# Attention kernel on one core: the queues of four engines in another planned order

## Chip, core and metric

The kernel runs on one core of a Trainium2 chip. The metric is the device time of one execution in microseconds (us), lower is better. A core has five engines with an instruction queue each, served in order: TensorE (PE, matmuls; PEld is its weight load), VectorE (DVE), ScalarE (ACT), GpSimd (POOL) and SyncE (SP, which here only issues transfers). They wait for each other through semaphores. On-chip data lie in SBUF; matmuls write to PSUM, which has eight banks.

## What is computed

Two attention blocks over S = 2048 positions, D = 1024, H = 32 heads of 32, whose outputs are concatenated:

```python
def _A_ref(x, wqkv, wo):
    qkv = ...                                   # x @ wqkv, split into heads
    scores = jnp.einsum('bhqd,bhkd->bhqk', q, k) * Dh ** (-0.5)
    p = _softmax(scores, axis=-1)
    o = jnp.einsum('bhqk,bhkd->bhqd', p, v)
    return o... @ wo

def _B_ref(x, wq, wk, wv, wo, beta):            # four segments of 512
    for s in range(N):
        logits = jnp.einsum('bhqd,bhkd->bhqk', qs, ks) * scale + mask
        a_dot = jnp.einsum('bhqk,bhkd->bhqd', _softmax(logits), vs)
        pq = phi(qs)
        a_mem = (pq @ M) / (pq @ z + 1e-06)
        o = g * a_mem + (1.0 - g) * a_dot
        M = M + jnp.einsum('bhld,bhle->bhde', phi(ks), vs)
        z = z + sum(phi(ks))
    return o @ wo
```

Block A is full attention; block B is causal attention within a segment plus a linear memory of the segments before.

## The kernel before

**The stream of scores.** Heads are worked on in groups of four (g = 0 to 7 in A). One score row (L1190) is a set of eight or more matmuls, four heads at once in four row tiles of TensorE, that fill four PSUM banks of 512 columns. Banks 0 to 5 form three slots of two; a row takes two slots and ScalarE empties each by one exp (`ACTIVATE P`, L1288). There are 593 pieces of rows and 1184 exps. For about a tenth of the tiles the exp is replaced by a square polynomial: VectorE reads the bank and scales it into Y (L1236, the cube read), GpSimd squares it (Z, L1245) and scales it into Pc (L1246). A row can start when the exps and cube reads of its banks' last contents are done.

**Work with the probabilities.** For each set TensorE multiplies P with V (L1401) and with ones for the row sums (L1408), in column tiles, into one bank of banks 6 and 7. VectorE then transposes the sums (L1515 or L1426), takes reciprocals (L1518), and GpSimd and VectorE scale and transpose the result back (L1533, L1535).

**Jobs.** Between rows TensorE does projections (L829 through `mm4`; L1866 for the first V), the memory of block B and the output products. A projection of a 512-column tile is eight steps over the contraction; each step is two operations of 256 columns (`halves`, L1593), which are emitted as one instruction of 512 columns if they stand next to each other in the queue. A job takes a bank of the pair 6 and 7 (`tenant`, L1576; the choice stands in the string `BANKS`, L26), VectorE evicts it (L1608) and squares it (L1621) for the bound that guards the exps. Changing between row tiles and column tiles is a change of `mode` in the program.

**Transfers.** All loads and stores but four go through SyncE's queue in program order; weights of block A's next pair of projections are loaded by L1544, x is loaded transposed by L1572.

**How the order is made.** `schedule` (L434) lists all operations with planned durations and puts them on five queues by keys, due times and readiness; its result is the starting order. `rearrange` (L606) then applies the table `MOVES` (L201), one string for TensorE, ScalarE, VectorE and GpSimd each. A pair `gap+shift` steps `gap` places on and takes the operation `shift` places behind to the place reached:

```python
for e, text in MOVES.items():
    q, i = queue[e], 0
    for gap, shift in (x.split("+") for x in text.split()):
        i += int(gap)
        q.insert(i, q.pop(i + int(shift)))
```

After it, the waits between tenants of one bank are derived from TensorE's order, and `programs` (L712) writes each queue with its semaphore waits. SyncE has no string, so its order stays that of `schedule`. Semaphore waits follow from the data dependencies, whatever the order.

Of the kernel before, what the change touches and what calls it, by code (L numbers as in the profile page):

```python
# [145 lines left out]
class Op:  # L146
# [17 lines left out]
    def __hash__(self):  # L164
# [50 lines left out]
        "9+1 12+1 1+1 1+1 1+1 1+1 2+8 2+7 5+1 1+1 9+1 4+5 1+5 1+5 1+5 1+6 1+6 1+6 1+6 1+6 1+6 1+5 19+1 1+1 1+1 1+1 2+2 2+1 1+1 "
        "1+1 1+1 1+1 1+1 1+1 1+1 1+1 1+1 1+4 1+1 1+1 1+1 1+1 1+1 1+1 13+11 3+9 1+9 1+2 9+1 6+1 1+1 1+1 1+1 5+1 8+3 1+3 9+18 1+18 "
        "1+18 5+2 12+1 7+2 1+2 1+2 1+3 1+3 1+3 1+2 1+2 1+2 1+2 1+2 1+2 1+2 1+3 1+3 1+3 1+3 1+2 9+1 1+1 1+1 1+1 1+1 4+10 1+10 1+10 "
        "1+10 1+10 1+10 1+5 2+8 3+6 5+3 10+1 1+1 1+1 1+1 1+3 12+5 9+1 1+1 2+5 1+4 1+4 1+4 1+4 1+4 1+4 1+4 1+4 1+4 1+4 1+4 1+4 1+6 "
        "1+4 1+4 1+4 1+4 11+1 1+1 1+1 1+1 1+1 1+1 1+1 1+1 1+1 1+2 1+2 1+5 1+1 1+4 1+4 1+4 1+4 16+1 1+2 1+2 1+2 1+2 3+2 1+2 1+2 "
        "1+2 1+2 1+2 1+2 1+2 2+3 10+1 1+1 1+1 1+1 5+5 1+5 1+5 9+1 1+1 12+1 1+1 1+2 2+1 1+1 1+1 1+1 1+1 1+1 2+2 1+17 12+4 3+3 7+3 "  # L220
        "3+3 7+1 12+7 1+7 1+7 1+5 12+3 11+2 5+2 8+2 1+2 1+2 1+2 1+2 1+2 1+2 1+2 1+2 1+5 1+2 1+2 1+2 1+2 1+2 1+2 1+2 1+2 6+5 1+5 "
        "6+4 1+4 1+4 1+4 1+4 1+5 1+4 1+4 1+4 1+4 1+4 1+4 1+4 1+4 1+4 1+4 1+4 3+4 3+4 5+2 1+2 1+2 1+2 1+2 1+2 1+1 1+1 1+1 1+1 1+1 "
        "1+1 1+1 1+1 1+2 1+2 1+5 2+1 1+1 1+1 4+3 1+3 1+3 1+3 1+3 1+3 3+1 1+1 3+1 1+1 1+1 1+1 1+1 1+1 1+1 1+1 1+1 1+1 1+1 1+1 4+1 "
        "1+1 7+3 2+2 1+2 1+2 1+2 3+5 1+5 3+1 1+1 2+3 1+3 1+3 1+3 2+1 2+1 1+1 1+1 1+18 1+1 1+1 1+1 1+1 1+1 1+1 1+2 1+2 2+1 1+1 1+1 "
        "1+1 1+1 1+1 1+1 1+1 1+1 1+1 1+1 1+1 1+1 2+7 1+7 1+7 1+7 4+4 1+4 1+4 1+4 2+5 1+3 1+3 1+3 1+3 1+3 1+3 2+2 1+2 6+4 2+4 1+4 "
        "1+4 1+4 1+4 1+4 5+3 14+3 5+1 1+1 1+1 1+1 1+1 1+1 2+3 8+3 6+3 5+1 1+1 2+3 3+1 1+1 1+1 1+1 1+1 1+1 1+1 1+1 1+1 1+1 1+4 1+1 "
        "1+1 1+1 1+1 1+1 1+5 7+1 5+4 1+4 1+4 1+4 1+5 1+5 1+5 1+4 1+4 1+4 2+3 1+3 1+3 1+3 2+2 1+2 1+5 6+5 1+5 1+5 1+5 6+4 13+4 6+3 "
        "1+3 1+3 1+3 1+3 1+3 1+5 1+3 1+3 1+3 1+3 1+3 1+3 1+3 1+3 1+3 1+3 1+6 9+1 2+5 7+13 1+13 3+7 7+4 5+5 5+1 4+17 1+17 4+4 14+2 "
        "13+3 3+4 3+2 1+2 1+2 1+2 1+2 2+5 5+1 1+1 1+1 5+7 1+5 5+2 1+2 1+2 1+2 1+2 1+2 1+2 1+2 1+2 1+2 5+1 1+2 1+2 1+2 1+2 11+1 "
        "1+1 1+1 1+1 1+1 1+1 1+1 1+1 4+1 1+1 1+1 1+1 1+1 1+1 1+1 4+4 1+4 1+4 1+4 1+4 1+4 1+4 1+4 1+4 1+4 3+1 2+7 1+7 1+7 4+1 1+1 "  # L230
        "1+1 1+1 1+1 1+1 1+1 3+2 1+2 1+3 3+1 1+1 1+1 1+1 1+1 1+1 4+1 1+1 1+1 1+1 1+1 1+1 10+5 1+5 1+5 1+5 1+1 1+4 1+4 1+5 1+5 3+3 "
        "1+3 13+1 1+1 1+1 1+1 1+1 6+13 1+1 1+1 1+12 1+12 12+1 1+1 9+1 1+1 13+1 1+1 5+2 1+2 1+2 1+2 1+3 1+3 1+2 1+2 1+2 11+1 6+3 "
        "4+3 12+5 11+5 1+10 7+5 1+5 1+5 1+4 1+4 1+4 1+4 1+4 1+4 1+4 1+4 1+4 1+4 1+4 1+4 1+4 1+4 1+4 10+4 1+3 2+3 1+3 1+3 1+3 1+3 "
        "4+12 2+11 2+1 12+1 14+1 6+1 1+1 7+1 1+1 13+1 2+3 1+3 1+3 1+3 1+3 1+3 4+1 7+3 1+3 1+3 1+3 1+3 8+4 1+4 8+14 1+18 1+18 13+7 "
        "1+7 1+7 1+7 1+7 1+7 5+4 1+4 1+2 1+3 1+3 1+3 1+3 1+3 1+3 1+3 1+3 1+2 6+4 1+4 1+4 1+4 1+4 1+4 1+5 1+5 2+6 1+6 1+6 1+6 4+1 "
        "1+2 1+2 2+1 1+1 3+1 1+1 1+1 1+1 1+1 1+10 1+10 8+1 1+1 1+1 1+1 8+1 1+1 1+1 1+1 1+1 1+1 1+1 2+5 1+5 1+5 1+5 1+5 1+5 2+4 "
        "1+4 1+1 1+3 1+3 1+3 1+4 1+4 1+4 1+4 1+4 7+5 1+5 1+5 1+5 2+4 1+4 1+1 3+1 1+1 1+1 1+1 1+1 1+2 1+2 1+2 1+2 1+2 7+1 1+1 1+1 "
        "1+1 1+1 2+15 1+15 1+15 9+1 7+1 1+1 1+1 1+1 1+1 10+9 1+10 1+10 1+10 15+1 1+1 1+1 1+19 1+19 2+18 1+18 11+1 9+1 1+18 1+18 "
# [2046 lines left out]
```

## Time and profile before

| | |
|---|---|
| median of 3 runs | 1057.38 us (1057.37 to 1058.42) |
| span of the profiled execution | 1056.3 us |
| mean granted TensorE clock | 1.000 |
| VectorE busy, idle in front of cube reads | 703.4 us, 110.1 us |
| GpSimd busy | 724.7 us |
| ScalarE: first and last exp | 11.9 us, 1043.6 us (end) |

In the profile's groups a row names the line, the engine, the operation and the tiles (output<-inputs), then busy time, mean duration in ns, and the idle time of the engine directly in front with what ended it. Rows of waits read "who <- for whom: us in total, times, longest"; they list the longer waits alone. Rows of the timeline give start, duration, engine, line, operation, and in brackets the idle time before. Matmuls overlap in the pipeline, so a duration there is longer than the distance to the next start.

### The profile page before, as it was taken

How to read it: one execution, taken by the hardware profiler on the slowest of the kernel's cores; microseconds unless marked ns; L12 is line 12 of the kernel's file. 1: busy time of each engine (PE TensorE's matmuls, PEld its weight loads, DVE VectorE, ACT ScalarE, POOL GpSimd, SP SyncE). 2: the span in 40 equal slices, each digit the busy share in tenths (PEclk: the TensorE clock that was granted, in tenths of full speed). 3: DMA queues.
4: the chain of work that ended last, by engine and by line, in shares of the span. 5: the costliest groups of instructions: out<-in, count | busy, mean ns of one | idle time of the engine just before them, and what ended most of it. 6: DMA issues, size and time to landing. Idle time of an engine off the chain costs nothing.

```text
span 1056.3 us, 54941 instructions
## 1 busy us (share of the span) xinstructions
PE 1023.3 (97%) x25091; PEld 551.2 (52%) x25092; DVE 703.4 (67%) x1451; ACT 1001.5 (95%) x1193; POOL 724.7 (69%) x999
## 2 busy tenths in 40 slices
PE   9999999999999999999999999999999999999998
PEld 4456455566555454556555445556555445445544
DVE  3457577666656878696755879777646887674444
ACT  5999999999999999898999999999999999999995
POOL 1005567666766888888956899888755878985551
PEclk9999999999999999999999999999999999999999
DMA  9213351007112530033241221133041433122002
GB/s 175 47 43 93 68 138 28 16 13 160 49 41 70 123 85 17 3 62 92 67 113 44 78 65 38 27 75 91 27 113 35 125 102 113 33 68 73 28 29 66
DMA packets 172377, 72.24 MB, mean 68 GB/s; under 512 B 135536, under 2 KB 170352, under 8 KB 172144
## 3 DMA queue, kind: packets, MB, share of 16 engines
q1 hardware_dynamic: 169776, 67.93, 26.3%
q8 instruction: 197, 3.23, 1.3%
q10 hardware_dynamic: 2368, 0.79, 0.3%
q14 instruction: 36, 0.29, 0.1%
HBM read 45.36 MB, written 11.80 MB: 54 GB/s over the span
## 4 chain that ended last, share of the span: by engine, by line
PE 56%; ACT 32%; DVE 4%; POOL 3%; SPq 3%; issue 1%; DMA 0%; ACTq 0%; POOLq 0%; DVEq 0%
ACT P L1288 32%; PE ps L829 27%; PE ps L1190 11%; PE ps L1401 8%; PE ps L1408 8%; SPq L1572 2%; POOL Z L1245 2%; DVE Y L1236 1%; PE ps L1866 1%; PE ps L1638 1%; POOL Pc L1246 1%; DVE T L1515 1%; DMA W_A<-in_A_wqkv_dram 0%; DVE PKQ_B L1925 0%; POOL P L1317 0%
## 5 line engine op out<-in xcount | busy, mean ns | idle before, releaser
L1288 ACT ACTIVATE P<-ps 128x1024 bf16<-128x1024 f32 (+1 forms) x1178 | 991.5, 999 | 33.6 <-PE ps L1190 18.7
L1245 POOL TENSOR_TENSOR Z<-Y 128x512 f32<-128x512 f32 x287 | 304.2, 1062 | 202.2 <-DVE Y L1236 177.7
L1408 PE MATMUL ps<-P,onesb 128*32 128x256 bf16 (+1 forms) x4386 | 300.8, 270 | 0.7 <-issue 0.6
L1401 PE MATMUL ps<-P,V_A 128*32 128x256 bf16 x3618 | 257.7, 274 | 0.7 <-issue 0.3
L1236 DVE TENSOR_SCALAR Y<-ps 128x512 f32<-128x512 f32 x239 | 163.7, 685 | 110.1 <-PE ps L1190 90.5
L1190 PE MATMUL ps<-KQ_A 32*128 32x256 bf16 x4096 | 204.1, 272 | 12.4 <-ACT P L1288 5.5
L1246 POOL TENSOR_SCALAR Pc<-Z 128x512 bf16<-128x512 f32 x239 | 155.6, 654 | 11.0 <-PE ps L1190 0.2
L1190 PEld LDWEIGHTS ps<-KQ_A 32*128 32x128 bf16 x4096 | 62.8, 92 | 163.9 <-ACT P L1288 108.7
L1408 PEld LDWEIGHTS ps<-P,onesb 128*32 128x32 bf16 x4386 | 128.8, 96 | 30.1 <-issue 14.8
L829 PE MATMUL ps<-xT_B,W_B 128*32 128x512 bf16 (+1 forms) x2132 | 138.7, 372 | 0.8 <-DVE OT_B L1948 0.2
L829 PE MATMUL ps<-xT_A,W_A 128*32 128x512 bf16 (+1 forms) x2020 | 131.4, 370 | 2.2 <-DMA W_A<-in_A_wqkv_dram 1.1
L1401 PEld LDWEIGHTS ps<-P,V_A 128*32 128x32 bf16 x3618 | 108.1, 96 | 34.3 <-issue 14.3
L1401 PE MATMUL ps<-Pc,V_A 128*32 128x256 bf16 x478 | 123.1, 273 | 0.4 <-ACT P L1288 0.2
L1408 PE MATMUL ps<-Pc,onesb 128*32 128x256 bf16 x478 | 122.8, 273 | 0.0
L1317 POOL TENSOR_SCALAR_AFFINE_SELECT P<-P 128x768 bf16<-128x768 bf16 (+1 forms) x96 | 76.3, 803 | 34.7 <-ACT P L1288 33.1
L1515 DVE STREAM_TRANSPOSE T<-ps 128x512 f32<-128x512 f32 x122 | 86.3, 708 | 14.0 <-PE ps L1408 11.9
L829 PEld LDWEIGHTS ps<-xT_B,W_B 128*32 128x32 bf16 x2132 | 50.3, 96 | 45.5 <-issue 19.6
L829 PE MATMUL ps<-Wo_B,OT_B 128*32 128x512 bf16 (+1 forms) x1080 | 71.6, 370 | 0.2 <-DVE rc L1518 0.2
L829 PE MATMUL ps<-Wv_B,xT_B 128*32 128x512 bf16 (+1 forms) x1096 | 70.3, 367 | 0.2
L829 PEld LDWEIGHTS ps<-xT_A,W_A 128*32 128x32 bf16 x2020 | 47.4, 96 | 42.1 <-issue 12.5
L1533 POOL TENSOR_TENSOR T<-T,rc 128x256 bf16<-128x256 f32 x74 | 48.9, 663 | 29.6 <-DVE rc L1518 25.8
L1608 DVE CAST KQ_A<-ps 128x512 bf16<-128x512 f32 x60 | 41.3, 689 | 40.5 <-PE ps L829 40.1
(109 smaller groups left out, 1201.0 us busy)
## 6 DMA issues: line engine op xcount, KB each, us to landing
Wv_B<-in_B_wv_dram SPq DMA_DIRECT2D x32, 256.0 KB, 3.5
W_B<-in_B_wk_dram SPq DMA_DIRECT2D x32, 256.0 KB, 3.3
W_B<-in_B_wq_dram SPq DMA_DIRECT2D x32, 256.0 KB, 4.1
Wo_B<-in_B_wo_dram SPq DMA_DIRECT2D x32, 256.0 KB, 3.5
out_dram<-outsb SPq DMA_DIRECT2D x56, 128.0 KB, 1.9
W_A<-in_A_wqkv_dram SPq DMA_DIRECT2D x14, 256.0 KB, 3.6
ot_a_scratch<-OTst SPq DMA_DIRECT2D x52, 64.0 KB, 2.3
xT_A<-ot_a_scratch SPq DMA_DIRECT2D x6, 512.0 KB, 4.8
```

The source lines that it names most:

```text
L829: ins = e.matmul(out[r], w[:, r], x, start=start, stop=stop, tile_position=(0, 32 * t), skip_group_check=True)
L1190: ins = e.matmul(out, kap, qap, start=st, stop=True, tile_position=(32 * h, 0), skip_group_check=True)
L1236: o = self.dve(lambda e: e.tensor_scalar(Y[:, :], src, SCALE, MID, ALU.mult, ALU.add), 512, key - 9.0, [self.bank[bank]], [rY], fixed=0.15)
L1245: self.pool(lambda e: e.tensor_tensor(Z[:, :], Y[:, :], Y[:, :], ALU.mult), 512, key, [rY], [rZ], rate=0.58)
L1246: return self.pool(lambda e: e.tensor_scalar(dst, Z[:, :], C2, REST, ALU.mult, ALU.add), 512, key, [rZ], [rP], rate=TS_RATE)
L1288: a = self.act(guarded if early and not free else lambda e: e.activation(dst, src, ACT.Exp, scale=SCALE), cols, key, rd, wr, fixed=EXP_FIXED)
L1317: self.pool(lambda e: e.affine_select(v, v, pattern=pat, compare_op=ALU.is_ge, fill=0.0, base=0, channel_multiplier=-1), 2 * nd * P, key + ...
L1401: ins = e.matmul(self.ps[32 * h:32 * h + 32, 512 * obk + q0:512 * obk + q0 + nq], v, p, start=first, stop=last, tile_position=(0, 32 * h), ...
L1408: ins = e.matmul(self.ps[32 * h:32 * h + 32, lcol + q0:lcol + q0 + nq], self.onesb[:, 0:32], p, start=False, stop=last, tile_position=(0, ...
L1515: self.dve(lambda e: e.transpose(T2[:, :], src), 512, k - NORM_K, [obk.res], [ro, rl], fixed=0.17)
L1533: self.pool(lambda e: e.tensor_tensor(half.rearrange("p (b r) -> p b r", r=32), ov, bc, ALU.mult), QC, k, [ro, rr], [rl], rate=0.435)
L1608: self.dve(lambda e: e.tensor_copy(dst, src), 512, key, [self.at(b)], rdst, fixed=0.155)
```

## The change

The diff has one hunk, the table `MOVES`. All four strings are replaced; the starting order, `BANKS`, every operation and the queue of transfers stay as they were. TensorE's string has 3135 moves where it had 3159, ScalarE's 16 for 26, VectorE's 1238 for 1195, GpSimd's 800 for 771. The first line of each:

```diff
 MOVES = {
     "PE": (
-        "14+1 1+2 1+3 5+1 5+1 6+1 1+3 1+1 1+2 4+3 2+1 3+1 1+3 2+1 1+3 1+4 5+1 1+1 1+1 1+1 1+1 1+1 1+1 1+1 1+1 1+1 1+1 1+1 1+1 1+1 "
...
+        "13+1 2+1 1+2 1+3 1+4 1+5 2+5 2+5 7+3 2+1 1+2 2+1 4+1 2+1 1+1 4+1 3+2 1+3 1+1 1+1 2+1 1+1 1+1 1+1 1+1 1+1 1+1 1+1 1+1 1+1 1+1 "
...
     "ACT": (
-        "6+1 7+3 24+1 1+1 1+1 1+1 1+1 1+1 1+1 1+1 1+1 1+1 1+1 1+1 1+1 1+1 1+1 52+1 1+1 1+1 1+1 1+1 1+1 1+1 1+1 1083+1 "
+        "6+1 9+1 22+1 1+1 65+1 1+1 1+1 1+1 1+1 1+1 1+1 1+1 1+1 1+1 1080+1 "
     ),
     "DVE": (
-        "1+1 1+1 9+1 1+2 15+2 1+1 2+2 4+1 1+1 1+1 1+4 1+1 1+1 2+1 2+1 1+3 1+1 1+1 3+1 2+1 1+1 1+1 1+1 1+6 1+6 1+2 1+5 1+5 1+5 1+8 "
...
+        "1+1 1+2 1+1 1+1 1+1 1+1 5+1 2+1 13+1 2+1 2+2 4+1 1+1 1+1 1+4 1+4 1+1 1+3 1+1 1+1 1+1 1+1 2+1 3+1 2+1 1+1 1+1 1+1 1+1 1+5 1+1 "
...
     "POOL": (
-        "19+2 1+2 6+1 1+1 2+2 2+1 2+1 4+1 1+1 5+2 3+1 2+1 3+1 1+1 3+1 1+1 1+1 5+1 5+3 1+3 1+5 1+3 1+5 1+3 2+4 1+3 1+2 1+3 1+2 4+6 "
...
+        "20+1 1+1 9+2 2+1 1+1 1+2 1+1 1+1 1+1 2+1 1+2 1+1 4+2 3+2 1+2 2+1 1+1 1+1 2+1 1+1 5+2 3+3 1+4 4+1 1+1 1+2 1+2 1+1 1+1 1+3 1+1 "
...
     ),
 }
```

As an example of what it does, TensorE's queue around the score row that starts at 31.78 us: before, the row is followed by four steps of the projection of K for pair 1 with a row-sum product and the last product with V of one set behind them; after, those products and one step of the projection stand in front of the row.

1 line of the change is left out of this document (added), and 339 rows, old and new, of the table MOVES.

## Prediction

> **What bounds the kernel now.** I read the page's busy shares first, then its chain of work that ended last, then the waits of TensorE and ScalarE, then the timeline at the longest of these waits.
>
> ```profile
> span 1056.3 us, 54941 instructions
> PE 1023.3 (97%) x25091; PEld 551.2 (52%) x25092; DVE 703.4 (67%) x1451; ACT 1001.5 (95%) x1193; POOL 724.7 (69%) x999
> PE 56%; ACT 32%; DVE 4%; POOL 3%; SPq 3%; issue 1%; DMA 0%; ACTq 0%; POOLq 0%; DVEq 0%
> L1288 ACT ACTIVATE P<-ps 128x1024 bf16<-128x1024 f32 (+1 forms) x1178 | 991.5, 999 | 33.6 <-PE ps L1190 18.7
> ...
> PE ps L1190 <- ACT P L1288: 7.7, 21, 0.8
> PE ps L1190 <- DVE Y L1236: 3.7, 9, 0.8
> PE ps L1401 <- DVE T L1515: 2.2, 10, 0.4
> PE ps L829 <- DMA W_A<-in_A_wqkv_dram: 1.1, 1, 1.1
> ...
> ACT P L1288 <- PE ps L1190: 18.7, 37, 1.2
> ACT P L1288 <- PE ps L1408: 11.6, 18, 1.6
> ```
>
> Two engines are nearly full and hand work to each other. TensorE is busy for 1023.3 of 1056.3 us, so all its idle time is 33.0 us, some of it the start and the end. TensorE's work ends only with the kernel's tail, so the span is its work plus its idle time: a new order can save the idle time and nothing else. The waits to look at stand in front of the score rows (L1190): 7.7 us where the exp (L1288) still reads the banks, 3.7 us where VectorE's cube read (L1236) does. The other direction, exps that wait for a row, is larger in sum but costs only what it passes on to TensorE. The execution shown has 1056.3 us from first to last instruction; the median of the runs is 1057.38, 1.1 more. I sum against 1056.3 and add 1.1.
>
> This is how a wait before a row looks (TensorE, then VectorE):
>
> ```profile
> 646.26 0.40 PE L1190 MATMUL ps<-KQ_A 32*128 32x256 bf16 x8
> 646.58 0.40 PE L829 MATMUL ps<-PKQ_B,Mb 128*32 128x512 bf16 x4
> 647.82 0.40 PE L1190 MATMUL ps<-KQ_A 32*128 32x256 bf16 x8 [0.83 <-DVE Y L1236]
> 648.14 0.29 PE L1401 MATMUL ps<-P,V_B 128*32 128x256 bf16 x4
> 648.26 0.28 PE L1408 MATMUL ps<-P,onesb 128*32 128x256 bf16 x4
> ...
> 647.02 0.65 DVE L1236 TENSOR_SCALAR Y<-ps 128x512 f32<-128x512 f32 x1
> ```
>
> The row at 647.82 may not overwrite its bank before the cube read ends at 647.67. One small matmul stood in front of it, and 0.83 us passed with nothing, although the product with V (L1401) and the row sums (L1408) at 648.14 come straight behind it.
>
> **The change part by part.** I played the old and the new table on the same starting queues and compared where each operation stands. No operation is added or removed. TensorE: 3590 of 7344 stand elsewhere; the 593 score rows keep their order. VectorE: 1099 of 1427; GpSimd: 777 of 995; ScalarE: 21 of 1196. The DMA queue on SyncE has no table, so no transfer passes another. BANKS is not in the diff, and each PSUM bank has the same tenants in the same order under both tables: "pool banks planned anew" has no counterpart, and costs and brings nothing.
>
> First term, waits that get work. Between 40 and 1040 us I find 67 score rows with a TensorE gap of over 20 ns in front, 14.6 us together (the 21 and 9 waits above are the longer ones). In the new order 31 of them have more work ahead, 9 less, 27 the same; over all 577 rows of that stretch it is 226, 160 and 191. So the work went where the trace idles, by 3.4 to 1 against 1.4 to 1. At 647.82, the product and row sums at 648.14 and 648.26 move in front: 0.22 us of the 0.83. Adding the smaller of gap and added work, row by row, gives 4.1 us. The other 70 gaps of TensorE (9.1 us, such as L1401 waiting for the transpose L1515) give 2.1 us in the same way. Term: -6.2 us.
>
> Second term, new waits. The 160 rows with less work ahead come earlier, by 30.7 us in sum, and may now meet a bank that is still being read. Taking for each the room it had between its bank's release and its start, and holding everything else, 6.7 us of new waits result; if the releases come earlier as well, none. For the releases: 50 exps stood over 0.2 us late behind their row, and 26 of those rows come earlier, 14 later, 4.7 us earlier in sum. An earlier exp frees its banks earlier, so I take 6.7 - 4.7 = 2.0, with 0 and 6.7 as ends. Term: +2.0 us.
>
> Third, TensorE's work itself.
>
> ```profile
> 26.07 0.28 PE L1408 MATMUL ps<-P,onesb 128*32 128x256 bf16 x4
> 26.18 0.28 PE L1401 MATMUL ps<-P,V_A 128*32 128x256 bf16 x4
> 26.39 0.40 PE L1190 MATMUL ps<-KQ_A 32*128 32x256 bf16 x8
> ...
> 29.11 0.28 PE L1408 MATMUL ps<-P,onesb 128*32 128x256 bf16 x4
> 29.22 0.28 PE L829 MATMUL ps<-xT_A,W_A 128*32 128x256 bf16 x4
> 29.33 0.28 PE L1401 MATMUL ps<-P,V_A 128*32 128x256 bf16 x4
> ...
> 23.57 1.04 PE L829 MATMUL ps<-xT_A,W_A 128*32 128x512 bf16 x16
> 24.54 0.40 PE L1190 MATMUL ps<-KQ_A 32*128 32x256 bf16 x8
> ```
>
> From start to start, four concurrent matmuls of 256 columns take 0.11 us (26.07 to 26.18), and 0.21 when a score row follows (26.18 to 26.39): a switch from column tiles to row tiles costs 0.10. The new order has 1199 such changes of tiling (both directions) for 1195, +0.4 us. Adjacent halves of a projection are emitted as one 512-column instruction; 95 pairs stand apart now, 179 after. Four wide quads take 24.54 - 23.57 less the switch, 0.87, that is 0.217 each, and two halves 2 x 0.11: 84 more split pairs cost 84 x 0.003 = 0.25 us, which their use as filler has to earn. Together +0.7 us.
>
> Fourth, the start.
>
> ```profile
> 30.52 0.72 PE L829 MATMUL ps<-xT_A,W_A 128*32 128x256 bf16 x12
> 31.78 0.40 PE L1190 MATMUL ps<-KQ_A 32*128 32x256 bf16 x8
> 33.24 1.05 PE L829 MATMUL ps<-xT_A,W_A 128*32 128x512 bf16 x16 [1.07 <-DMA W_A<-in_A_wqkv_dram]
> 34.88 0.40 PE L1190 MATMUL ps<-KQ_A 32*128 32x256 bf16 x8
> ...
> 28.09 1.21 SPq L1544 DMA_DIRECT2D W_A<-in_A_wqkv_dram  x2
> ...
> 21.21 13.20 ACT L1288 ACTIVATE P<-ps 128x1024 bf16<-128x1024 f32 x14
> 35.32 5.60 ACT L1288 ACTIVATE P<-ps 128x1024 bf16<-128x1024 f32 x6 [0.91 <-PE ps L1190]
> ```
>
> The weights of pair 1 are issued at 28.09 and used at 33.24 after a wait of 1.07. In the new order one wide quad of that projection stands in front of the score row that now starts at 31.78. The transfer keeps its place, so the row is held to 33.24 + 0.22 + 0.10 = 33.56, and its exps start 0.44 later (34.88 to 35.32), at 34.00. The exps before them end at 34.41 less two of 13.20/14 = 0.94, that is 32.52: a hole of 1.5 us in ScalarE, of which the old hole of 0.91 falls away (next row at 33.56 + 0.33 + 13 x 0.11 = 35.3, exps ready behind those of the held row). Late by 0.5 us; behind all of it stand the later rows' exps. If the weights land 1.5 us sooner it costs nothing; if the hole is added whole, 1.5. Term: +0.5 us.
>
> The moves on the other engines I cost at nothing.
>
> ```profile
> 58.68 0.30 ACT L1671 ACTIVATE braw<-bias 128x1 f32<-128x1 f32 x1
> ...
> out_dram<-outsb SPq DMA_DIRECT2D x56, 128.0 KB, 1.9
> ```
>
> On ScalarE the factor at 58.68 goes 13 places forward, to about 46 us, with the same 0.30 us. On GpSimd the farthest move, 178 places, is a copy of two columns that the next segment reads. Evictions on VectorE feed 56 output transfers on SyncE's queue, and a late one would hold the loads behind it; behind 40 us no TensorE wait above ends with a transfer, and that room covers it. If it is gone, a late eviction costs what it is late, up to 0.7, one more VectorE instruction like the cube read below (163.7/239 = 0.69).
>
> Sum: -6.2 + 2.0 + 0.7 + 0.5 = -3.0, a span of 1053.3, and **1054.4 us** for the median. With no new waits and no loss at the start it is 1056.3 - 6.2 + 0.7 = 1050.8, 1051.9 with the 1.1; with all new waits and the whole hole, 1056.3 - 6.2 + 6.7 + 0.7 + 1.5 = 1059.0, 1060.1.
>
> **The rivals.** *The waits move and stay in sum.* TensorE's rows only keep pace with ScalarE, so work brought ahead of a row is missing before a later one. For it: 27 of the 67 waiting rows have the same work ahead, and the longest waits for an exp are among them. Against it: the 160 rows that lose work are mostly rows without a gap. New waits and the start's hole then equal the fill, 6.2, and the 0.7 of work remains: a span of 1057.0, 1058.1 for the median.
>
> *Slower: the cube reads come late.* A row cannot start before VectorE has read its bank, and VectorE serves in order.
>
> ```profile
> L1236 DVE TENSOR_SCALAR Y<-ps 128x512 f32<-128x512 f32 x239 | 163.7, 685 | 110.1 <-PE ps L1190 90.5 <-PE ps L829 7.3 <-POOL Z L1245 6.1
> L1621 DVE TENSOR_TENSOR sqB<-KQ_B 128x512 bf16<-128x512 bf16 x64 | 37.6, 593 | 0.2
> L1621 DVE TENSOR_TENSOR sqA<-KQ_A x64: 377/419/1149, 10.8 to 841.1; 128x512 bf16<-128x512 bf16 x64
> DVE Y L1236 <- PE ps L1190: 90.5, 94, 2.6
> PEld ps L1190 <- DVE Y L1236: 16.6, 47, 0.5
> L1245 POOL TENSOR_TENSOR Z<-Y 128x512 f32<-128x512 f32 x287 | 304.2, 1062 | 202.2 <-DVE Y L1236 177.7
> ```
>
> In the new order 43 of the 239 cube reads have a square (L1621) ahead that stood behind, 20 the reverse. 94 reads come after idle time of 90.5/94 = 0.96 us, which covers a square; for the others, 43 x 145/239 = 26 reads, it delays. The weight loads of 47 rows in 239 stand directly behind a cube read, one in five: 26/5 = 5 rows x 0.59 = 3.1 us. With the first rival's balance that is 1058.1 + 3.1 = **1061.2 us**; it decides once more than about five tight reads (3.0/0.59) are delayed. The squares last 377 to 1149 ns, so at the upper end it is 5 x 1.15 = 5.8 and 1063.9. The Trainium skill (SBUF — State Buffer, Who interferes with whom) says that VectorE's instructions with two SBUF inputs and GpSimd's reads exclude each other through a shared port; the trace's spread of 377 to 1149 ns agrees, beside GpSimd multiplications of 1062. By that rule a square put ahead of a read can last as long as a multiplication, and it would be the upper end. Against this rival: over all cube reads, VectorE work ahead grew for 91 and shrank for 106.
>
> **How the numbers follow.** This kernel's measurement tells about 0.2% (2.1 us) from no change, so the limits are 1055.3 and 1059.5. Forecast, the fill outlasts the new waits: 0.47, its own range 1051.9 to 1057. Waits move, 1058.1: 0.21. Cube reads late, 1061.2: 0.32. The forecast's case lies near the limit, and 0.04 of it falls within 0.2%; of the second case 0.17 lies within and 0.04 above; of the third 0.02 within and 0.30 above. Faster 0.43, same 0.23, slower 0.34. The range: from 1051.0, 0.9 under the forecast's best sum, to 1062.0, between the third case and its upper end; about 0.2 is left outside.
>
> **What would show it.** Right: TensorE's waits before L1190 fall from 11.4 us (7.7 + 3.7) to 8 or less, the row at 647.82 waits about 0.6, TensorE's busy time stays within 1 us of 1023.3, and the wait for the first weights now holds a score row, with a longer ScalarE hole at 33 us. Wrong by the first rival: the sums of waits are the same with other places. Wrong by the second: "L1190 <- DVE Y" grows past 6 us, with squares in front of those reads. A saving with no loss of waits, or a changed busy time of TensorE, would show that the span is not its work plus its waits, and the sum's basis would fall.

## The result and the profile after

The changed kernel takes 1062.22 us (median of 4 runs, 1061.62 to 1064.45); the kernel before took 1057.90 in its 4 runs beside it. The ratio is 1.0042, 95% interval 1.0028 to 1.0056: slower by 4.3 us. The execution shown has a span of 1060.24 us, 4.0 over the 1056.25 before. In the changed kernel every line number below the tables is 5 lower (L1190 is L1185, L1288 is L1283, L1236 is L1231).

These are the page's totals, and waits of TensorE and ScalarE (who <- for whom: us in total, times, longest):

```profile
span 1060.2 us, 55629 instructions
PE 1024.7 (97%) x25428; PEld 558.6 (53%) x25428; DVE 697.1 (66%) x1451; ACT 1001.8 (94%) x1193; POOL 724.7 (68%) x999
...
PE ps L1185 <- ACT P L1283: 10.4, 26, 1.1
PE ps L1396 <- issue: 1.9, 2, 1.3
PE ps L1396 <- DVE T L1510: 1.8, 7, 0.5
PE ps L824 <- DVE KQ_B L1603: 1.4, 4, 0.9
...
PE ps L824 <- issue: 0.7, 2, 0.4
PE ps L1185 <- DVE Y L1231: 0.7, 2, 0.4
...
ACT P L1283 <- DVE flags L1713: 2.5, 1, 2.5
```

Four things are to be seen. The listed waits in front of score rows are 10.4 + 0.7 = 11.1 us where they were 7.7 + 3.7 = 11.4: other releasers, the same sum. Waits ended by "issue" are new in size: TensorE stood still although nothing the profile shows held it. One ScalarE wait of 2.5 us for the guard's flag was not there before. And projections (L824) wait 1.4 us for VectorE's eviction of KQ_B, where the row before was

```profile
PE ps L829 <- DVE KQ_B L1608: 0.2, 1, 0.2
```

TensorE's idle time grew from 33.0 to 35.5 us.

**Where the time went.** Starts of the same score row in two traces can't be compared directly, since the new order puts another amount of work in front of a row. So I subtract from the difference of the starts the difference of TensorE's work ahead of that row, each group of four matmuls at its usual distance to the next start (0.109 us, 0.2165 for 512 columns, 0.105 for a change of tiling). What is left is the corrected lag against the kernel before; it moves only where one kernel waits and the other doesn't. (The changes of tiling are those between row tiles and column tiles. With those to and from the undivided array, `128*128` in the rows, the lag of the changed kernel is some 0.3 us lower from 238 us on.) In us, with five of the experiments below:

```
at us          43    238    265    430    490    654    710    821    852    880    907   1041
changed     -0.50  -1.46  -0.26  -0.04   0.15   0.80   1.69   1.79   2.88   4.23   4.14   4.22
f2_join     -0.21  -1.03   0.13   0.24  -0.14   0.83   1.79   2.09   3.39   3.70   3.97   4.18
e4_shift     3.23   2.74   2.90   2.85   3.11   4.19   5.07   5.15   5.54   5.31   5.28   5.35
g1_head     -0.39  -1.12  -0.95  -0.90  -1.27  -0.59   0.09   0.10   0.13   0.57   0.57   0.57
f1_fill     -0.31  -0.36  -0.06  -0.05  -1.05  -0.98  -0.89  -0.74  -0.79  -0.81  -0.91  -0.91
f4_bshift    0.05   0.31   1.75   1.77   1.38   1.64   1.65   1.69   1.70   2.00   2.42   2.42
```

The changed kernel is 1.46 us ahead at 238 us. It loses 1.2 us from there to 265, 0.9 from 654 to 710, 1.1 from 821 to 852 and 1.35 from 852 to 880, the rest in small steps. Two of these losses have a face in the trace. At 882 us TensorE stops in the middle of one group of four matmuls:

```profile
880.33 0.27 PE L1396 MATMUL ps<-P,V_A 128*32 128x256 bf16 x1
881.89 0.29 PE L1396 MATMUL ps<-P,V_A 128*32 128x256 bf16 x3 [1.30 <-issue]
```

The four share one operation and its inputs; the first ran, the other three 1.56 us later. At 850 us the guard's flag is late, and with it the eviction behind it on VectorE's queue (VectorE, then GpSimd, ScalarE and TensorE):

```profile
847.50 0.65 DVE L1231 TENSOR_SCALAR Y<-ps 128x512 f32<-128x512 f32 x1
...
848.29 0.15 DVE L1713 SCALAR_TENSOR_TENSOR flags<-braw,flags 128x1 int32<-128x1 f32 x1
848.36 1.01 DVE L1705 SCALAR_TENSOR_TENSOR bias<-braw 128x1 f32<-128x1 f32 x1
...
849.65 0.41 DVE L1713 SCALAR_TENSOR_TENSOR flags<-braw,flags 128x1 int32<-128x1 f32 x1
849.98 0.68 DVE L1603 CAST KQ_B<-ps 128x512 bf16<-128x512 f32 x1
...
848.30 1.04 POOL L1240 TENSOR_TENSOR Z<-Y 128x512 f32<-128x512 f32 x1
849.43 0.62 POOL L1241 TENSOR_SCALAR Pc<-Z 128x512 bf16<-128x512 f32 x1
...
850.53 3.35 ACT L1283 ACTIVATE P<-ps 128x1024 bf16<-128x1024 f32 x4 [2.45 <-DVE flags L1713]
...
850.80 0.83 PE L824 MATMUL ps<-xT_B,W_B 128*32 128x512 bf16 x12 [0.88 <-DVE KQ_B L1603]
```

The cube read at 847.50 stands in front of the guard's last steps in both orders. In the new order of GpSimd its end releases the multiplication at once, at 848.30 (before, the cube read of 845.26 us had its multiplication only at 849.62), and the write of one element per partition at 848.36 takes 1.01 us, until that multiplication ends. The flag is written at 850.06 and the exp starts behind it. What TensorE itself waits for, 0.88 us, is the eviction of KQ_B, which VectorE starts behind the flag; the corrected lag grows by the same 0.88 at the next row. Whether the flag alone would have cost as much was not tested. In the kernel before no such multiplication ran beside these steps:

```profile
846.12 0.15 DVE L1718 SCALAR_TENSOR_TENSOR flags<-braw,flags 128x1 int32<-128x1 f32 x1
846.19 0.15 DVE L1710 SCALAR_TENSOR_TENSOR bias<-braw 128x1 f32<-128x1 f32 x1
...
846.62 0.16 DVE L1718 SCALAR_TENSOR_TENSOR flags<-braw,flags 128x1 int32<-128x1 f32 x1
```

By the rule of the Trainium skill (SBUF — State Buffer, Who interferes with whom) VectorE's instructions with two inputs in SBUF and GpSimd's instructions that read SBUF exclude each other through a shared port; the trace agrees, 0.15 us alone and 1.01 beside a multiplication of 1.04.

### The profile page after: what moved, and what is told of

It reads as the page before. It is cut to its first block, busy times and chain, and to the rows that moved or that the text cites. A ratio compares the mean times of both kernels' runs of the same rounds, so it can differ in the third digit from the quotient of the medians.

```text
span 1060.2 us, 55629 instructions
## 1 busy us (share of the span) xinstructions
PE 1024.7 (97%) x25428; PEld 558.6 (53%) x25428; DVE 697.1 (66%) x1451; ACT 1001.8 (94%) x1193; POOL 724.7 (68%) x999
## 3 DMA queue, kind: packets, MB, share of 16 engines
q8 instruction: 200, 3.28, 1.3%
## 4 chain that ended last, share of the span: by engine, by line
PE 55%; ACT 38%; DVE 4%; POOL 1%; issue 1%; SPq 0%; DMA 0%; ACTq 0%; POOLq 0%; DVEq 0%
ACT P L1283 37%; PE ps L824 26%; PE ps L1185 11%; PE ps L1396 8%; PE ps L1403 7%; PE ps L1861 1%; POOL Z L1240 1%; PE ps L1633 1%; DVE T L1510 1%; ACT P L1261 0%; SPq L1567 0%; DVE KQ_B L1603 0%; DVE Y L1231 0%; DVE KQ_B L2104 0%; DMA xT_A<-in_A_x_dram 0%
## 5 line engine op out<-in xcount | busy, mean ns | idle before, releaser
L1283 ACT ACTIVATE P<-ps 128x1024 bf16<-128x1024 f32 (+1 forms) x1178 | 991.9, 1010 | 38.4 <-PE ps L1185 19.9
L1403 PE MATMUL ps<-P,onesb 128*32 128x256 bf16 (+1 forms) x4386 | 308.7, 270 | 0.0
L1396 PE MATMUL ps<-P,V_A 128*32 128x256 bf16 x3618 | 264.5, 274 | 2.4 <-issue 1.9
L1231 DVE TENSOR_SCALAR Y<-ps 128x512 f32<-128x512 f32 x239 | 164.4, 688 | 113.4 <-PE ps L1185 95.6
L1185 PE MATMUL ps<-KQ_A 32*128 32x256 bf16 x4096 | 204.0, 273 | 11.8 <-ACT P L1283 7.6
L1185 PEld LDWEIGHTS ps<-KQ_A 32*128 32x128 bf16 x4096 | 62.0, 92 | 155.9 <-ACT P L1283 92.5
L824 PE MATMUL ps<-xT_B,W_B 128*32 128x512 bf16 (+1 forms) x2212 | 142.8, 365 | 1.5 <-DVE KQ_B L1603 0.9
L824 PE MATMUL ps<-xT_A,W_A 128*32 128x512 bf16 (+1 forms) x2084 | 134.0, 364 | 0.8 <-DVE KQ_A L1603 0.2
L824 PE MATMUL ps<-Wo_B,OT_B 128*32 128x512 bf16 (+1 forms) x1180 | 76.2, 352 | 0.4 <-DVE outsb L1603 0.4
L824 PEld LDWEIGHTS ps<-xT_B,W_B 128*32 128x32 bf16 x2212 | 53.4, 96 | 43.5 <-issue 17.9
L824 PE MATMUL ps<-Wv_B,xT_B 128*32 128x512 bf16 (+1 forms) x1128 | 72.6, 361 | 0.3 <-DVE KQ_B L1603 0.2
L824 PEld LDWEIGHTS ps<-xT_A,W_A 128*32 128x32 bf16 x2084 | 49.9, 96 | 39.7 <-issue 12.9
L1603 DVE CAST KQ_B<-ps 128x512 bf16<-128x512 f32 x64 | 44.1, 689 | 32.7 <-PE ps L824 32.3
```

The source lines that it names most:

```text
L824: ins = e.matmul(out[r], w[:, r], x, start=start, stop=stop, tile_position=(0, 32 * t), skip_group_check=True)
L1185: ins = e.matmul(out, kap, qap, start=st, stop=True, tile_position=(32 * h, 0), skip_group_check=True)
L1231: o = self.dve(lambda e: e.tensor_scalar(Y[:, :], src, SCALE, MID, ALU.mult, ALU.add), 512, key - 9.0, [self.bank[bank]], [rY], fixed=0.15)
L1283: a = self.act(guarded if early and not free else lambda e: e.activation(dst, src, ACT.Exp, scale=SCALE), cols, key, rd, wr, fixed=EXP_FIXED)
L1396: ins = e.matmul(self.ps[32 * h:32 * h + 32, 512 * obk + q0:512 * obk + q0 + nq], v, p, start=first, stop=last, tile_position=(0, 32 * h), ...
L1403: ins = e.matmul(self.ps[32 * h:32 * h + 32, lcol + q0:lcol + q0 + nq], self.onesb[:, 0:32], p, start=False, stop=last, tile_position=(0, ...
```

## Experiments

A longer table or an added line moves the line numbers of the experiments by 39 to 44 against the kernel before; the rows below are recognised by their operation. Ratios are to the kernel before, run beside each, with the 95% interval.

### One engine's order alone

```diff
 MOVES = {
     "PE": (...
 e1_pe, in the changed kernel:
-    "DVE": (new table), "POOL": (new table)
+    "DVE": (table of before), "POOL": (table of before)
 e2_vec, in the kernel before:
-    "DVE": (table of before), "POOL": (table of before), "ACT": (table of before)
+    "DVE": (new table), "POOL": (new table), "ACT": (new table)
```

> The changed kernel with the earlier orders of VectorE and GpSimd; TensorE (and ScalarE) keep the new order. Theory 1 (the waits in front of the score rows kept their sum; what was lost lies in a few places: the guard's flag at 850 us late by 1.0 us through VectorE's and GpSimd's order, one stall of 1.3 us of TensorE at 882 us and 0.95 us of such stalls at 253 and 265 us that belong to TensorE's stream, and 1.4 us more work of TensorE): about 1.0 us under the changed kernel, 1061.2 us, with the flag back at its old place and stalls without a wait still near 2.8 us in sum. Theory 2 (the forecast's step 1 holds, work put ahead of the waits gains, and the new VectorE order takes it away): 1055 us or less. Theory 3 (TensorE's order alone loses): 1062 us or more.

> The kernel before with the new orders of VectorE and GpSimd (and ScalarE's); TensorE keeps the earlier order. Theory 1: the late flag comes along if it hangs on these two engines (+1.0 us), the stalls of TensorE's stream don't (1.24 us in sum as before): about 1059 us. Theory 2: the loss lies in the new VectorE order, so 1061 us or more. Theory 3: as the kernel before, 1058 us, within 0.5 us.

Measured: e1_pe 1071.46 us, 1.0135 (1.0115 to 1.0155); e2_vec 1066.30 us, 1.0081 (1.0068 to 1.0094). No theory holds for both runs: theory 3 had e1_pe at 1062 or more and missed e2_vec, theory 2 had e2_vec at 1061 or more and missed e1_pe, theory 1 missed both. Each half of the change alone is far worse than both kernels. TensorE's waits, first of e1_pe, then of e2_vec, show what breaks:

```profile
PE ps L1440 <- DVE T L1554: 5.1, 13, 1.5
```

```profile
PE ps L1444 <- DVE T L1558: 3.9, 13, 1.1
```

The products with V wait for VectorE's transposes for 5.1 and 3.9 us, against 2.2 before and 1.8 after. The tables look like one plan: an operation moved on TensorE needs its eviction moved on VectorE. These longer waits are 3 us and 2 us of a loss of 14 and 9; the rest was not taken apart. So no single engine can be blamed from these two. The guard's operations take 0.15 and 0.16 us in e1_pe; in e2_vec the last of them takes 0.66 beside a multiplication, so the collision comes with the orders of VectorE and GpSimd. The stall at 882 us went with TensorE's order: e1_pe shows it at the same instruction, between the first and the second of the same four matmuls,

```profile
887.75 0.27 PE L1440 MATMUL ps<-P,V_A 128*32 128x256 bf16 x1
889.39 0.29 PE L1440 MATMUL ps<-P,V_A 128*32 128x256 bf16 x3 [1.37 <-issue]
```

while e2_vec, with the old stream, has 0.34 us inside a score row at 883.87.

### The late flag

```diff
     def rearrange(self, queue):
 ...
+        queue["POOL"][807].deps.add(queue["DVE"][1185])
```

> The changed kernel with one more wait: the GpSimd multiplication of L1240 that started at 848.30 us waits until VectorE has written the second guard flag, so that the small VectorE operations of L1705 and L1713 (1.01 and 0.41 us there, 0.15 and 0.16 in the kernel before) run without GpSimd beside them. Theory 1: these two fall back to 0.15 to 0.2 us, the flag lands about 1.0 us earlier against the score row before it, and the time falls by 1.0 us to about 1061.2. Rival (what is saved there is lost at the next wait of ScalarE or TensorE, since sums of waits hold): the flag is early but the time stays at 1062.2 within 0.3.

Measured: 1061.30 us (7 runs), 1.0031 (1.0020 to 1.0043). VectorE and ScalarE at the place:

```profile
849.65 0.14 DVE L1761 SCALAR_TENSOR_TENSOR flags<-braw,flags 128x1 int32<-128x1 f32 x1
849.71 0.15 DVE L1753 SCALAR_TENSOR_TENSOR bias<-braw 128x1 f32<-128x1 f32 x1
...
850.14 0.16 DVE L1761 SCALAR_TENSOR_TENSOR flags<-braw,flags 128x1 int32<-128x1 f32 x1
...
850.78 5.18 ACT L1331 ACTIVATE P<-ps 128x1024 bf16<-128x1024 f32 x6 [1.26 <-PE ps L1451]
```

The two small operations take 0.15 and 0.16 us, ScalarE's wait falls from 2.45 to 1.26 and ends with TensorE, and TensorE's wait of 0.88 us for the eviction is gone. From 840 to 859 us the corrected lag grows by 0.32 us here and by 1.08 in the changed kernel. So the collision is shown to cost 0.8 us at the place; the median is 0.9 lower, which the intervals of the two kernels don't separate. The span of the execution shown is nevertheless the changed kernel's, 1060.2 us. It had been 1.3 us ahead at 823 us and was 1.4 behind at 844: at 830.85 us TensorE stood for 0.99 us, ended by "issue", where the changed kernel with the same stream did not, and from 831.5 to 834.9 us the granted clock was 0.5. In the windows the columns are the span of the window, busy time of PE, PEld, DVE, ACT and POOL, granted clock, DMA share and GB/s; first the changed kernel, then e3_flag:

```profile
820.00:840.00 20.00, 18.75 (x440) 9.22 (x432) 17.59 (x38) 18.66 (x23) 17.88 (x26) 1.00 0.48 138
```

```profile
820.00:840.00 20.00, 18.16 (x392) 8.51 (x392) 15.57 (x32) 16.55 (x20) 15.45 (x24) 0.91 0.48 137
```

### The stream of TensorE's instructions

```diff
-WARM = 13
+WARM = 13; NSPLIT = 9
 ...
-                self.fill = self.pe(lambda e: e.matmul(self.ps[:, 512 * 5:512 * 6], dummy[:, 0:P], dummy[:, :], start=True, stop=True), dur,
+                self.fill = self.pe(lambda e, m=8 if key == -99.5 and _ < NSPLIT else 1: [e.matmul(self.ps[:, 512 * 5 + 512 // m * i:512 * 5 + 512 // m * (i + 1)], dummy[:, 0:P], dummy[:, 512 // m * i:512 // m * (i + 1)], start=True, stop=True) for i in range(m)][-1], dur,
```

The same edit on the changed kernel (e4_shift) and on the kernel before (f4_bshift).

> The changed kernel with 63 more pairs of weight load and matmul in front: 9 of the 13 warm-up matmuls of 512 columns become 8 of 64 columns each, so that every later instruction of TensorE stands 126 places further in its stream, half of one 16 KB block of 256 instructions, while all orders and waits stay. If the stalls of TensorE without a wait (2.85 us in five places, 1.30 at 881.9) come from blocks of instructions that arrive late, they move or go: the one at 882 us falls under 0.5 us or stands elsewhere, and the time changes by -1 to +1 us along with their sum. If they come from anything else (the clock, the matmuls, a wait that the trace does not show), they stand at the same instructions with the same length and the time stays at 1062.2 within 0.4.

> The kernel before with the same 63 more pairs of weight load and matmul in front. Its five stalls without a wait (1.24 us in sum, 0.62 at 485.9 and 0.31 at 477.2) should move. If stalls of the stream count in full, the time changes by what their sum changes: between -1.2 us (none left, 1056.4) and +1.6 us (as many as in the changed kernel, 1059.2). If they are made up at the next wait for ScalarE, the time stays at 1057.6 within 0.4 whatever their sum.

Measured: e4_shift 1062.95 us, 1.0044 (1.0028 to 1.0061); f4_bshift 1060.06 us, 1.0016 (1.0005 to 1.0028). In e4_shift no TensorE wait ends with "issue" any more; the group at 882 us, now at 882.99, runs whole:

```profile
882.99 0.28 PE L1443 MATMUL ps<-P,V_A 128*32 128x256 bf16 x4
```

Behind 43 us its corrected lag grows by 5.35 - 3.23 = 2.1 us, that of the changed kernel by 4.22 + 0.50 = 4.7. But this execution is 3.7 us late at 43 us. The windows show that place, here e4_shift, then the changed kernel:

```profile
20.00:30.00 10.00, 8.82 (x207) 6.16 (x208) 5.16 (x13) 9.74 (x12) 0.00 (x0) 1.00 1.04 150
30.00:40.00 10.00, 9.30 (x192) 4.88 (x192) 3.16 (x5) 6.75 (x8) 0.00 (x0) 0.83 0.40 86
```

```profile
20.00:30.00 10.00, 9.92 (x238) 6.80 (x239) 5.01 (x13) 9.74 (x13) 0.00 (x0) 1.00 1.18 187
30.00:40.00 10.00, 9.66 (x256) 5.52 (x248) 4.05 (x9) 10.00 (x13) 0.00 (x0) 1.00 0.14 25
```

Between 20 and 30 us TensorE was busy for less, with waits for transfers of xT_A of 1.8 us in sum; between 30 and 40 us the granted clock was 0.83, since it was 0.5 from 32.2 to 35.6 us. Why the transfers came late here is open.

Apart from the last 5 us of each trace, one such stretch of 3.4 us at a clock of 0.5 stands in five of the fifteen traces: e1_pe (945.9 us), e3_flag (831.5), e4_shift (32.2), f3_all (32.4) and g2_loads (937.6). In e3_flag four concurrent matmuls of 512 columns followed the four before after 0.43 us there, not 0.2165. In g2_loads the rows went from 0.70 us ahead of the changed kernel's to 0.48 behind, 1.2 us for the stretch. These five executions have a mean granted clock of 0.998 or less, the ten others of 0.999 or more. By that mark 17 of the 51 executions of the seven kernels with TensorE's new order all through (the changed one, e1_pe, e3_flag, e4_shift, f2_join, f3_all, g2_loads) have such a stretch, 1 of the 91 of the kernel before that ran beside the experiments, and 4 of the 77 of the other seven kernels; why the new order meets it more often is open. It does not make the changed kernel's loss: three of its four executions have none, and their median is 1062.04 us. But it hides what e4_shift gained: 1060.58, 1060.60 and 1062.51 us for the three executions without it, 1063.38 to 1064.91 for the three others. That split was made after the fact and the executions are few.

In the kernel before, the edit brought stalls in:

```profile
PE ps L870 <- issue: 1.9, 2, 1.1
...
PE ps L1231 <- issue: 0.8, 1, 0.8
...
PE ps L1449 <- issue: 0.3, 1, 0.3
```

3.0 us in sum where the kernel before had 1.24, and the median rose by 2.1 us with every order unchanged. This is what shows that such stalls count about in full.

### Bulk loads and blocks of instructions

```diff
     def rearrange(self, queue):
 ...
+        for i, j in [(286, 6091), (289, 6114), (290, 6141), (291, 6159), (292, 6195)]:
+            queue["SP"][i].deps.add(queue["PE"][j])
```

> The changed kernel with all orders kept; five of the 512 KB loads of xT_A that ran between 870 and 881 us, and what follows them on SyncE's queue, each wait for a score row, so that they start near 874, 877, 882, 885 and 890 us instead of back to back (their first use is at 901 to 903 us). TensorE's stream is the same instruction for instruction. If its stall at 882 us is a block of instructions that comes late behind those loads, the stall falls under 0.3 us, the spacing of 9.0 us between blocks there falls to about 6, and the time falls by about 1.3 us to 1060.9. If the stall comes from the stream's phase alone, whatever the loads do, it stays at 1.0 to 1.4 us and the time at 1062.2.

Measured: 1061.63 us, 1.0032 (1.0019 to 1.0045). What the DMA engines did from 871 to 879.5 us (packets, MB, share of 16 engines), in the changed kernel and then here; q8 carries blocks of instructions:

```profile
DMA packets 978, 2.16 MB, mean 254 GB/s; under 512 B 99, under 2 KB 355, under 8 KB 978
...
q1 hardware_dynamic: 978, 2.16, 77.0%
...
xT_A<-ot_a_scratch SPq DMA_DIRECT2D x4, 512.0 KB, 6.9
```

```profile
DMA packets 752, 1.34 MB, mean 158 GB/s; under 512 B 79, under 2 KB 335, under 8 KB 750
...
q1 hardware_dynamic: 750, 1.31, 50.1%
q8 instruction: 2, 0.03, 1.7%
...
880.67 0.27 PE L1445 MATMUL ps<-P,V_A 128*32 128x256 bf16 x1
881.20 0.29 PE L1445 MATMUL ps<-P,V_A 128*32 128x256 bf16 x3 [0.26 <-issue]
```

In the changed kernel no block of instructions came in these 8.5 us, but one at 870.66, just ahead of them, and one at 879.64; with the loads spread they came at 871.12 and 878.75. So the spacing fell from 9.0 to 7.6 us, not to the 6 expected, and the same instruction waits 0.26 us in place of 1.30. It is matmul 21301 of the stream, counted from 0, and waits 1.37 us in e1_pe and 0.96 in e3_flag, where the loads stand as in the changed kernel. So at this place the loads are the cause of most of the stall. The time fell by 0.6, not 1.3; five of the eight executions have a clock of 0.998, and the one shown lost the 1.2 us named above at 937.6. It also had stalls of 0.62 and 0.83 us at 245 and 254 us, where the changed kernel, with the same stream, had 0.56 and 0.39 at 253 and 265 us and e3_flag 0.13 at 245: how blocks and loads meet varies between executions. The sums vary less, 2.85, 2.4 and 2.5 us in the changed kernel, e3_flag and g2_loads, 1.24 and 1.3 in the kernel before and g6_pace.

```diff
+        for i, j in ((85, 1903), (86, 1927), ... (292, 6219)):
+            queue["SP"][i].deps.add(queue["PE"][j])
```

These are 18 loads of SyncE's queue, each with a score row; g5_headpace has them on g1_head, the kernel with the new tables up to 238 us (below), g6_pace on the kernel before.

> The new order for what the kernel before runs up to 238 us and the earlier one behind it, as in the run with that seam, and 18 bulk loads (of W_A, Wv_A, Wv_B, xT_B and xT_A, around 260, 487, 690 to 716 and 870 to 890 us) that each wait for a score row, so that they start about 4 us apart and not back to back; what is loaded, in which order, and the instruction stream of TensorE stay. If TensorE's stalls without a wait come from bulk loads in front of its instruction blocks, the stalls at 694 and 875 us go and those near 456 and 490 stay or shrink, the lead of about 1 us that the seam kept up to 440 us is kept to the end, and the time is 1056 to 1057. If they come from the stream alone, they stay and the time is that of the run without the pacing, 1059.4.

> The kernel before with the same 18 loads paced in the same way, no order changed. Stalls without a wait of the kernel before stand at 247, 477, 486 and 865 us (1.08 us in sum behind the start); only the loads near 487 and from 870 us on are paced beside them, so at most some 0.6 us go: 1057 to 1057.6. If the pacing itself costs (data late for the projections that use it), the time is over 1058 and rows near 285, 512, 730, 764 or 900 us wait for a transfer.

Measured: g5_headpace 1059.54 us, 1.0012 (1.0003 to 1.0020); g6_pace 1058.57 us, 1.0001 (0.9990 to 1.0011). In g5_headpace the corrected lag stays at 1.32 from 613 to 840 us and at 1.87 from 866 us to the end: no stall at 694 or 875 us, where g1_head lost 0.6 and 0.45. But it had lost 0.7 us at 255 us and 0.54 at 849, at loads that were not paced, so the time is that of g1_head. In g6_pace the stall of 0.62 near 486 us stood, the pacing cost nothing.

### The fill by itself

f1_fill is the kernel before with 28 of the moves on TensorE; one of them in emission order:

```diff
+pv 455
+l 455
 score row 232
 ...
-pv 455
-l 455
```

> The kernel before with one part of the change alone: in front of 28 score rows that wait in the profile of before (5.35 us of waits in sum), TensorE work that the change also puts ahead of them, and whose inputs were there in time, is moved from just behind the row to just ahead of it (5.65 us of work, 3.95 us of it inside the waits). Nothing else moves on any engine. Forecast's step 1 (the fill is gained, the rows behind cost only a part of it): the waits in front of score rows fall by 3 to 4 us in sum and the time to 1054 to 1055. Rival (the work is missing in front of the next rows, which ScalarE's pace sets): the 28 waits shrink, rows that had none wait instead, the sum stays within 1 us and the time within 0.7 us of the kernel before.

Measured: 1056.89 us (12 runs), 0.9989 (0.9978 to 0.9999). The 28 waits fell from 5.35 to 1.76 us; all other rows waited 12.41 us where it was 9.73. How a gain is lost is seen at row 232, first before (start, duration), then here:

```profile
414.32 0.40 PE L1190 MATMUL ps<-KQ_A 32*128 32x256 bf16 x8
...
415.73 0.40 PE L1190 MATMUL ps<-KQ_A 32*128 32x256 bf16 x8 [0.32 <-ACT P L1288]
...
417.69 0.40 PE L1190 MATMUL ps<-KQ_A 32*128 32x256 bf16 x8
...
420.80 0.40 PE L1190 MATMUL ps<-KQ_A 32*128 32x256 bf16 x8
```

```profile
414.49 0.40 PE L1231 MATMUL ps<-KQ_A 32*128 32x256 bf16 x8
...
415.89 0.40 PE L1231 MATMUL ps<-KQ_A 32*128 32x256 bf16 x8
...
417.73 0.40 PE L1231 MATMUL ps<-KQ_A 32*128 32x256 bf16 x8
...
420.97 0.40 PE L1231 MATMUL ps<-KQ_A 32*128 32x256 bf16 x8
```

The row stands 1.40 us behind its neighbour, not 1.41, although 0.22 us of work went in front of it: ScalarE sets its start. The next row comes 0.12 us sooner (1.84 for 1.96), the one at 420.97 later again, with a wait of 0.15, and the sum over the four rows is 6.48 for 6.48. Of the 28 places the traces show 25 by work and wait. There the corrected lag falls at the row by about what was filled, and at 21 of the 25 it is back to within 0.05 us at one of the next four rows; the other four keep 0.10 to 0.17. What f1_fill gains on the kernel before comes from two other places: 0.3 us in front of the first rows, and about 0.8 us at 477 to 504 us, where the stalls of before are smaller.

### Half quads, both repairs, and splices

```diff
 MOVES = {
-    "PE": (new table: 179 pairs of halves apart)
+    "PE": (the same order with 141 of them joined)
```

> The changed kernel with 141 of its 179 split pairs joined again (the second half of a projection's quad follows the first at once, as one instruction of 512 columns), 38 stay apart; the kernel before has 95 apart. All else keeps the new order. If split pairs cost 0.003 us each, as the prediction put it, 0.4 us are gained and waits may come instead: 1061.5 to 1063. If the 1.4 us by which TensorE's busy time grew come from the 84 more split pairs (0.017 us each), busy time falls by 2.4 us and the time to about 1060. The stream of TensorE's instructions is shorter by about 1100, so stalls without a wait will stand at other places.

> The changed kernel with both repairs at once: GpSimd's multiplication waits for the second guard flag (alone 1061.3), and the 63 more pairs of weight load and matmul in front that moved TensorE's stream by half a block (alone no stall without a wait, 1062.95 over executions with a granted clock of 0.995 to 1.0, 1060.6 to 1062.5 where it was 1.0). Theory 1 (late flag 1.0 us and stalls 1.6 us more than before): 1059.8, with executions at a clock of 1.0 at 1059 to 1060. Rival (the sums of waits hold, so that a repaired wait comes back): 1062 within 0.5.

Measured: f2_join 1061.89 us, 1.0037 (1.0023 to 1.0050), busy time of TensorE 1025.0 us; f3_all 1060.43 us (12 runs), 1.0021 (1.0010 to 1.0032). Joining the halves changes nothing, so they are not where busy time grew. f3_all recovers 1.8 us of the 4.3 by the medians; the intervals just overlap. The execution shown, at 1063.33 the slowest of the 12, is late at the start by 3.6 us, as e4_shift was and with the same stretch at half the clock; the median of the ten executions without one is 1060.28. Its corrected lag grows by 2.0 us behind 43 us; with one stall of 0.18 us left and the flag repaired, these 2.0 are neither.

g1_head takes all new tables up to 238 us and the old ones behind; g3_best the new ones in seven stretches.

> All four engines in the new order for what the kernel before runs up to 238 us, and in the earlier order from there. Compared row by row, with the difference of TensorE's work ahead of a row taken off, the changed kernel was 1.46 us ahead at 238 us and lost only behind it. Theory 1 (what the new order gains or loses in front of a row is settled there and stays): the lead of 1.2 to 1.5 us is kept to the end and the time is 1056.5, give or take what stalls of TensorE's stream without a wait change against the 1.24 us of the kernel before. Rival (a gain is borrowed: ScalarE or TensorE waits for it later): the lead is gone by some 100 us behind the seam and the time is 1058 within 0.4.

> Spliced from both orders: for all four engines the new order in seven stretches where, row by row and with TensorE's work ahead taken off, it gained in five kernels that use it (22.8 to 40.7, 79.6 to 219, 344.7 to 387.7, 604.3 to 624.7, 801.9 to 812.4, 857 to 888.7 and from 955.1 us; -5.0 us in sum), and the earlier order between them. Theory 1 (gains are settled where they are made): 1053 to 1055 us, plus what stalls without a wait add against 1.24 us. Rival (gains are borrowed and come back as waits behind each seam): 1057 to 1058.

Measured: g1_head 1059.41 us, 1.0017 (1.0004 to 1.0030); g3_best 1061.10 us, 1.0032 (1.0021 to 1.0042). In g1_head the lead of 1.1 us at 238 us is 0.9 us at 430: it is kept over 190 us and was no loan. It goes at 456, 694 and 875 us, and TensorE's waits there are ended by "issue":

```profile
PE ps L1229 <- issue: 0.9, 3, 0.5
```

g3_best loses 1.3 us at its seam at 219 us and has 2.9 us of stalls; it tells little of the rest.

No kernel tried beats the kernel before by more than f1_fill, and that by 0.1%.

## Why the prediction was wrong

It said 1054.4 us; 1062.22 came, just over the upper end of the range, 1062.0. By its terms:

1. **Waits that get work, -6.2: held for the rows, failed for the other gaps.** Counted in both traces from 40 to 1040 us, with the work between a row and the row before it, 33 of the 67 waiting rows have more work ahead. They wait 3.0 us where it was 8.3: -5.3, for 4.1 expected. The row at 647.82 was to wait 0.6; it waits 0.27. The 2.1 us from TensorE's other gaps did not come. Without the stalls these gaps were 9.0 us and are 10.6: +1.6 in place of -2.1. What grew are the waits for VectorE's evictions (KQ, V, OT, outsb): 2.9 us before and 5.3 after, and 2.7 in f4_bshift and g6_pace, 4.4 to 5.3 in e3_flag, e4_shift, f2_join, f3_all and g2_loads.
2. **New waits, +2.0: this step failed.** The 510 rows that had no wait now have 3.85 us (0.14 before), of it 2.7 on those with less work ahead; the other 34 waiting rows are up by 1.3: 5.0 in place of 2.0. In sum 14.70 us became 14.44. The step took 4.7 us off the 6.7 for releases that come earlier. The sum of the waits shows no such gain. My reading is that an exp follows the exp before it, and the row follows the exp; f1_fill shows it alone: work put into such a wait is missing within four rows. The first rival had this right.
3. **TensorE's work, +0.7.** Counted with the distances above, 0.33 us, and 0.55 with the two more changes to or from the undivided array that the traces show; f2_join shows no cost of halves. TensorE's busy time grew by 1.4 us. Another reason is at hand: a group of four matmuls is shown for 0.28 us and followed after 0.11, so a wait of up to 0.17 us in front of the next one is covered by the modelled end and counts as busy. Busy plus idle is the span, but busy is not work, and the sum's basis, work plus idle time, falls with that. The Trainium skill (Perfetto Trace Analysis, Identifying the Most-Contended Engine) says that the busy share of matmuls is not a good measure of how close TensorE is to its limit, because matmuls are pipelined; the trace agrees with 1.4 us of busy time for 0.55 of work.
4. **The start, +0.5.** The weights were issued at 27.07 us, not 28.09, the row behind them was not held, and the lag is -0.5 at 43 us. The prediction had this as its other case.
5. **Moves on the other engines, 0: failed for VectorE and GpSimd.** The prediction looked for late evictions in front of transfers. What came late was the flag and the eviction behind it: GpSimd's multiplication, taken earlier than before, ran beside the guard's steps, 1.1 us from 821 to 852 us, 0.8 of it removed by e3_flag. The size depends on which step the multiplication meets: in e4_shift and f2_join, with the same orders of VectorE and GpSimd, TensorE waits 0.39 and 0.32 us there, not 0.88. The later evictions of point 1 belong here too.
6. **What had no term.** Stalls by late blocks of instructions were 1.24 us before and 2.85 after, +1.6. The change has 336 more matmuls of TensorE and as many weight loads in its stream, for which three more blocks are loaded, and blocks fall due at other moments. That they are due to the loads in front is shown at 882 us; that they count is shown by f4_bshift.

The span tells the same by terms, measured against forecast: rows -0.3 for -2.1, other gaps +1.6 for -2.1, stalls +1.6 for nothing, busy time +1.4 for 0.7, the first 40 us and the end -0.3 for +0.5; in sum +4.0 for -3.0.

Of the corrected 4.2 us, 1.6 are stalls, 1.1 the flag, -0.5 the start. The remaining 2.0 are waits that outweigh: 1.0 gained from 43 to 238 us and 3.0 lost behind, of it 0.9 from 654 to 710 us, the same in all kernels with the new order. There the waits are many and short, mostly under 0.3 us. In f3_all, with flag and stalls repaired, the waits for evictions are still 1.5 us over those before; that they make the rest was not tested, and which moves make them stays open.

The first rival was right on the sum of the rows' waits, but its 1058.1 us lacks the stalls, the flag and the evictions. The second came near in time, 1061.2, for a wrong reason: waits for cube reads fell from 3.7 to 0.7 us.

## What to carry to other kernels

Where two engines pace each other, a filled wait is a gain only if the work is not missing before the other engine's next hand-over; move one wait's work alone and follow the lag over the next rows before counting it. Compare two orders by starts corrected for the work ahead, not by sums of idle or busy time. And where a kernel is tuned to a few tenths of a per cent, an edit that changes the length of an engine's code can change the sum of its stalls by as much (here by 2.9 and 1.8 us), so an edit that only shifts the code belongs beside each comparison, and the granted clock of every execution is to be read before medians are compared.

## What was not expected of the hardware

TensorE's instructions arrive in blocks of 16 KB over the same DMA engines as the data (200 blocks, 3.28 MB in the changed kernel, 197 before), usually some 5 us apart. When 2.16 MB of loads filled 77% of the engines' time, a block came 9.0 us after the one before, and TensorE stood for 1.30 us in the middle of an operation. 63 more pairs of instructions in front removed all such stalls from one kernel and raised them from 1.24 to 3.0 us in another.

The granted clock fell to 0.5 for 3.4 us in some executions, at 32, 831, 938 or 946 us, and cost 1.2 us in g2_loads. Read by the mean clock of the executions, that was 17 of 51 with the new order of TensorE and 1 of 91 with the order before.
